# Paired steps on VectorE, streamed output weights and pooled weights transposed off TensorE in an attention + rational MLP kernel

## The chip, the cores and the metric

The kernel runs on one core of a Trainium2 chip. The metric is the device time of one execution in microseconds; the kernel before takes 930.41 us as the median of three runs (929.94 to 931.01). Engines are named as in the profile: PE is TensorE, PEld its weight loads, DVE is VectorE, ACT is ScalarE, POOL is GpSimd, SP is SyncE, which here only issues DMAs.

## The reference

Inputs are q, k, v of shape (8 batches, 8 heads, 576 tokens, 64), a 512x2048 matrix w_in, a 2048x512 matrix w_out and six coefficients. Everything is float32. Cut to what matters:

```python
# attention: a pooled part and a narrow local part, added
q_d, k_d, v_d = means of q, k, v over groups of 4 tokens          # 144 of 576
out_up    = repeat(softmax(q_d k_d^T / 8) v_d, 4)                 # back to 576
out_local = softmax(where(|i - j| < 4, q k^T / 8, -1e9)) v        # band of width 7
x = (out_up + out_local), heads side by side                      # 4608 x 512
# rational MLP
h = x @ w_in                                                      # 4608 x 2048
P = a0 + a1 h + a2 h^2 + a3 h^3
Q = 1 + |b0| |h| + |b1| h^2
out = (P / (Q + 1e-6)) @ w_out                                    # 4608 x 512
```

## The kernel before, in words

**The two products.** The 4608 tokens are cut into nine blocks of 512: blocks 0 to 7 hold the first 512 tokens of one batch each, block 8 the last 64 of all eight. A block has 16 steps; step n (0 to 143) computes h for 128 of the 2048 hidden columns. Float32 accuracy comes from splitting each operand into a high part that TensorE's one-pass float32 format holds and a low rest: three products (high x high, low x high, high x low) of four 128x512 matmuls, 12 per step (`h_part`, line L1389; in steps 0 to 15 it is four plain float32 matmuls instead, L1375). `middle(n)` turns the 128x512 h in PSUM into g and splits it: ScalarE reads h four times, VectorE runs seven operations of 512 columns (L1419 to L1437), ScalarE forms the reciprocal as exp(-ln Q) between them. `o_part(n, f)` multiplies g with 128 rows of w_out, again 12 matmuls (L1455), into four PSUM banks, one per 128 tokens, which gather all 16 steps of a block. `store` copies the four banks to SBUF, into the room of the block's high x (`xsf[blk.slot][0]`), and sends them out. So w_in and w_out stay in SBUF as high and low parts for the whole run, 16 tiles of 512 KB for each matrix.

**The attention** of batch b + 2 runs beside block b + 1. It goes by halves of a batch (`Half`: four heads as two pairs). Local scores of ten windows of 58 queries, a band mask, softmax; the local weights are transposed by VectorE (`flip`, L1129) from batch 2 on. VectorE's transpose works inside 32x32 blocks, so the blocks are brought to their partitions by four DMAs out to DRAM (`fd`, L1141) and one back (`ef`, L1146). Pooled scores use means of q and k (`pq`) that the DMA queues form: one load on SyncE (L524) and three that add on GpSimd's queue (L528); pooled values (`vpc`) come the same way. The pooled weights are transposed by TensorE, nine 112x112 transposes per half (`turn_pooled`, L1158) into PSUM, and ScalarE copies them out (L1170). `weight_both` (L754, L1209) multiplies all weights with v in one run of small matmuls, VectorE adds the two parts into x, and `split_x` makes its high and low part in four ScalarE and four VectorE operations per block.

**The order.** All work is handed to a list planner (`Plan`): each task has an engine, a cost, what it reads and writes, and a due time (`due_h(n)` for step n, with offsets such as `O_LAG`, `ENDS`, `SCORES_EARLY`). `Plan.run` gives each engine's free time to the open task with the earliest latest start, and the resulting order is written into the engines' queues; each queue keeps that order on the chip. `middle(n)` works in six tiles `mt` and four `gt`, two sets in turn:

```python
ta, tb, tq = (mt[2 * i + n % 2] for i in range(3))
gh, gl, u, log = rooms_g(n)
```

Of the kernel before, what the change touches and what calls it, by code (L numbers as in the profile page):

```python
# [2 lines left out]

# [25 lines left out]
QR = D + QC  # L29
BAND0 = 48  # L30
# [58 lines left out]
class Task:  # L89
    __slots__ = (  # L90
        "engine", "dur", "fn", "due", "preds", "succs", "late", "start", "end", "n", "lag", "uses", "load", "after",
        "loan", "step", "takes",
# [3 lines left out]
class Plan:  # L96
# [12 lines left out]
    def add(self, engine, dur, fn, reads=(), writes=(), due=None, lag=None, load=0.0, after=0.0):  # L109
# [4 lines left out]
        t.loan = next((w for w in writes if isinstance(w, Loan)), None) if engine == "PE" else None  # L114
        t.step = None
# [52 lines left out]
    def run(self):  # L168
        self.low, self.lent = 0, {}
        for t in reversed(self.tasks):  # L170
            late = 1e9 if t.due is None else t.due
            for s in t.succs:
                late = min(late, s.late - t.dur - self.gap(t, s))
            t.late = late
# [99 lines left out]
def attention_moe(  # L274
# [10 lines left out]
    band: bass.AP,  # L285
    out: bass.AP,
# [55 lines left out]
    mt = [put(f"m{i}", [P, DM], F32) for i in range(6)]  # L342
    gt = [put(f"g{i}", [P, DM], F32R) for i in range(4)]
    gb = [put(f"gb{i}", [P, DM], F32, g.at) for i, g in enumerate(gt)]
    ident = put("ident", [P, P], F32)
    identb = put("identb", [P, P], BF16)
    maskb = put("maskb", [P, 2, NW // 2 * D], BF16)
    maskd = put("maskd", [P, 2, NW // 2, QD], BF16)
# [9 lines left out]
    class Slot:  # L358


        def __init__(self, i, at=None):
# [8 lines left out]
            self.pq = one("pq", [P, 2, SD])  # L370
# [7 lines left out]
    class Pooled:  # L378


        def __init__(self, i, at=None):
            self.e = put(f"epc{i}", [P, NQ, NK, 2, D], F32, at)
            self.et = put(f"eptc{i}", [QR, NK * NQ, 2, QC], F32, self.e.at)
            keys = sorted(self.e.keys)
            self.rooms = [Room(None, keys[j::2]) for j in range(2)]

    pools = [Pooled(0)]
    slots = [Slot(i) for i in range(2)]
    vpc = put("vpc", [QR, 2, NK, D], F32)

# [17 lines left out]
    ]  # L408
    bounce = [[nc.dram_tensor(f"fd{i}_{j}", [4, QD, 4, NW // 2 * QD], F32, kind="Internal").ap() for j in range(2)] for i in range(2)]
# [44 lines left out]
    def weights(w, f, spot, due=None):  # L454
# [26 lines left out]
        if w or f >= NAT:  # L481
            parts(w, f)

# [10 lines left out]
    class Pair:  # L494
# [11 lines left out]
        def ep(self, i):  # L506
            return self.pool.e.ap[:, i, :, self.odd, :QC]

# [8 lines left out]
    def load_pooled(cs, values):  # L517

        b, q = cs[0].b, cs[0].i // 2
        loads = [(c.slot.pq, 0.5, [qkp[b, r, :, c.i] for r in range(POOL)]) for c in cs]  # L520
# [60 lines left out]
    def scores_pooled(cs, bk):  # L581
        def issue():
            for i in range(NQ):
                for n, c in enumerate(cs):
                    pq = flat(c.slot.pq.ap)
                    for j in range(2):
# [3 lines left out]
                            lhsT=pq[js, i * QC : i * QC + D],  # L590
                            rhs=pq[js, SD:],
# [3 lines left out]
        add("PE", 0.9 if cs[0].b == 0 else 1.15, issue, [c.slot.pq for c in cs], bk)  # L595
# [60 lines left out]
    def softmax_pooled(c, x, head=True):  # L656
# [17 lines left out]
        def exps():  # L674
            for i in range(NQ):
                nc.scalar.activation(  # L676
                    out=c.ep(i), in_=view[:, i, :].rearrange("p (n k) -> p n k", k=QC), func=AF.Exp,
# [151 lines left out]
    class Half:  # L829
# [22 lines left out]
        def scores(self, c, bk):  # L852
# [21 lines left out]
            add("PE", 0.95, issue, (c.slot.qk,), bk, due=self.due - SCORES_EARLY[c.odd] if c.b >= LATER else None)  # L874
# [22 lines left out]
        def scores_rest(self, bk):  # L897
# [21 lines left out]
            def pooled(i, j):  # L919
                js = slice(j * D, (j + 1) * D)  # L920
                for n, c in enumerate(self.cs):
                    pq = flat(c.slot.pq.ap)
                    nc.tensor.matmul(
                        bk[c.pos(j)].ap[n * D : (n + 1) * D, i * SD : (i + 1) * SD],
                        lhsT=pq[js, i * QC : i * QC + D],
                        rhs=pq[js, SD:],
# [3 lines left out]
            def issue():  # L930
# [17 lines left out]
                "PE", SREST, issue, (o.slot.qk, *(c.slot.pq for c in self.cs)), (*bk, bc),  # L948
                due=self.due - SCORES_EARLY[1]
# [78 lines left out]
        def pooled(self, bk):  # L1028
# [5 lines left out]
            if self.cs[0].b >= FLIP:  # L1034
# [3 lines left out]
                for c in self.cs:  # L1038
                    normalize(c, "pooled")
                return  # L1040
# [112 lines left out]

        def turn_pooled(self, bk):
# [27 lines left out]
        def weight_both(self, bk):  # L1182
# [15 lines left out]
            def issue():  # L1198
# [5 lines left out]
                for kc in range(NK):  # L1204
                    for h in range(2):
                        ks = slice(h * D, h * D + QC)
                        for n, c in enumerate(self.cs):
                            j = c.pos(h)
                            nc.tensor.matmul(  # L1209
                                bk[n].ap[j * D : (j + 1) * D, np_ : np_ + SD],  # L1210
                                lhsT=vpc.ap[ks, n, kc, :],
                                rhs=self.pool.et.ap[ks, kc * NQ : (kc + 1) * NQ, n, :],
# [7 lines left out]
            ready = [vpc, self.pool.et] + [c.slot.vw for c in self.cs] + [  # L1220
# [96 lines left out]
    def split_x(k, due=None):  # L1317
        blk = blocks[k]
        due = due or due_h(blk.first) - SPLIT_EARLY
        t = blk.t  # L1320
        for c in range(NCC):
            if blk.b is None:
                hi, lo = (tails(x, c) for x in blk.x)
                x = tails(xsf[blk.slot][1], c).ap
            else:
                hi, lo = (part(x, x.ap[:, c, :], 4 * c * t, 4 * t) for x in blk.x)
                x = xsf[blk.slot][1].ap[:, c, :]
            add("ACT", 0.11 + t / 1390, lambda hi=hi, x=x: nc.scalar.copy(out=hi.ap, in_=x), (lo,), (hi,), due=due)
            add(
                "DVE", 0.07 + t / 960,  # L1330
                lambda hi=hi, lo=lo, x=x: nc.vector.tensor_tensor(
                    out=lo.ap, in0=x, in1=hi.ap.bitcast(F32), op=ALU.subtract
                ),
                (lo, hi), (lo,), due=due,
            )
# [14 lines left out]
    def rooms_g(n):  # L1350
        k = n - blocks[-1].first
        k = k % 6 if k >= 0 else n % 2
# [52 lines left out]
    def middle(n):  # L1405

        ta, tb, tq = (mt[2 * i + n % 2] for i in range(3))
        gh, gl, u, log = rooms_g(n)
# [6 lines left out]
        read.append(act(0.66, gh, h, h.ap, AF.Identity, to=u, scale=a1, bias=a0))  # L1415
        v = nc.vector
        add(
            "DVE", 0.66,
            lambda: v.scalar_tensor_tensor(  # L1419
# [394 lines left out]
```

## Time and profile before

| what | value |
|---|---|
| runs, median (lowest to highest) | 930.41 us (929.94 to 931.01) |
| profiled execution, first to last instruction | 928.5 us |
| PE busy | 916.7 us (99%), 7129 matmul records |
| DVE busy | 859.7 us (93%) |
| ACT busy | 785.5 us (85%) |
| POOL busy | 117.7 us (13%) |
| DMA | 100.24 MB, mean 108 GB/s |
| granted TensorE clock | 1.00 |

The profiled execution's own time is its span; the page gives no time around it. Busy time is the union of an engine's instructions. The plain float32 matmuls of steps 0 to 15 have two records each. Small matmuls in different quarters of the array overlap, so their count says little; the time from one start to the next does.

### The profile page before, as it was taken

Reading aid. Unit: us, or ns where it says so; the run is one execution under the profiler, and the core shown is the slowest. Engines: PE = TensorE matmul, PEld = TensorE weight load, DVE = VectorE, ACT = ScalarE, POOL = GpSimd, SP = SyncE. Lnnn points to the kernel's source line nnn. Section 1 sums busy time; section 2 is a strip of 40 time slices with the busy share of each in tenths; the row PEclk is TensorE's granted clock in tenths of the full one; section 3 lists DMA queues with packets and bytes.
Section 4 is the critical chain, followed back from the end, with each engine's and each line's share of the span. In section 5 each row is a group of like instructions: output and inputs, shape, how many; then the busy total and the mean of one; then the engine's idle time right before and its main releaser. Section 6 shows DMA issues by size and latency. Waiting matters only on the chain.

```text
span 928.5 us, 19329 instructions
## 1 busy us (share of the span) xinstructions
PE 916.7 (99%) x7129; PEld 727.8 (78%) x7129; DVE 859.7 (93%) x1409; ACT 785.5 (85%) x1898; POOL 117.7 (13%) x140
## 2 busy tenths in 40 slices
PE   8999999999999999999999999999999999999998
PEld 6666667788888888788888888888888888888886
DVE  8899999999999998999999999999999989988994
ACT  5899997978897979888898979797989887678782
POOL 3122021202020202020112112021200000000000
PEclk9999999999999999999999999999999999999999
DMA  9987453636363634464455436463622110001001
GB/s 315 328 270 187 138 133 96 145 88 131 97 159 99 133 93 114 102 134 95 122 108 140 79 87 164 105 129 81 143 78 53 30 46 1 1 0 46 1 1 45
DMA packets 61853, 100.24 MB, mean 108 GB/s; under 512 B 8064, under 2 KB 41920, under 8 KB 61760
## 3 DMA queue, kind: packets, MB, share of 16 engines
q1 hardware_dynamic: 43888, 78.93, 26.6%
q0 software_dynamic: 17728, 19.96, 15.3%
q8 instruction: 56, 0.92, 0.4%
q14 instruction: 37, 0.30, 0.1%
q10 hardware_dynamic: 144, 0.13, 0.0%
HBM read 81.69 MB, written 17.30 MB: 107 GB/s over the span
## 4 chain that ended last, share of the span: by engine, by line
PE 75%; ACT 10%; DVE 10%; issue 3%; DMA 1%; SPq 0%; DVEq 0%; ACTq 0%
PE psum L1455 34%; PE psum L1389 33%; ACT m L1403 3%; ACT gb L1403 1%; PE psum L754 1%; ACT el L648 1%; DVE g L1428 1%; DVE m L1431 1%; ACT epc L676 1%; DVE m L1436 1%; DVE m L1419 1%; PE psum L1158 1%; PE psum L1209 1%; PE psum L1375 1%; PE psum L911 1%
## 5 line engine op out<-in xcount | busy, mean ns | idle before, releaser
L1455 PE MATMUL psum<-wh,g 128*128 128x512 f32 x1072 | 367.3, 403 | 2.7 <-DVE g L1428 1.4
L1389 PE MATMUL psum<-xs,wh 128*128 128x512 f32 x1024 | 256.9, 391 | 0.2 <-DVE xf L804 0.2
L1403 ACT ACTIVATE m<-psum,cf 128x512 f32<-128x512 f32 x288 | 217.4, 760 | 44.8 <-PE psum L1389 37.3
L1455 PEld LDWEIGHTS psum<-wh,g 128*128 128x128 f32 x1072 | 200.0, 188 | 54.8 <-issue 5.7
L1389 PEld LDWEIGHTS psum<-xs,wh 128*128 128x128 f32 x1024 | 191.0, 188 | 40.9 <-DVE xf L804 0.7
L1455 PE MATMUL psum<-wl,g 128*128 128x512 f32 x536 | 209.3, 390 | 0.0
L1389 PE MATMUL psum<-xs,wl 128*128 128x512 f32 x512 | 137.1, 390 | 0.0
L1403 ACT ACTIVATE gb<-psum,cf 128x512 f32<-128x512 f32 x134 | 109.7, 819 | 16.4 <-PE psum L1455 15.5
L1403 ACT ACTIVATE gb<-m,cf 128x512 f32<-128x512 f32 x134 | 101.7, 759 | 21.1 <-DVE m L1419 16.3
L1455 PEld LDWEIGHTS psum<-wl,g 128*128 128x128 f32 x536 | 100.7, 188 | 22.1 <-issue 2.3
L1428 DVE TENSOR_TENSOR g<-m,m 128x512 fp32r<-128x512 f32 x134 | 92.3, 689 | 23.4 <-ACT m L1403 17.3
L1389 PEld LDWEIGHTS psum<-xs,wl 128*128 128x128 f32 x512 | 96.0, 188 | 20.0
L1419 DVE SCALAR_TENSOR_TENSOR m<-m,cf,m 128x512 f32<-128x512 f32 x144 | 107.3, 745 | 2.4 <-ACT m L1403 2.1
L528 POOL DMA_DIRECT2D pq<-in_qkp_dram x84 | 75.9, 958 | 218.4 <-DMA pq<-in_qkp_dram 178.2
L1403 ACT ACTIVATE m<-gb 128x512 f32<-128x512 f32 x134 | 89.1, 665 | 14.7 <-DVE m L1424 12.5
L1436 DVE TENSOR_TENSOR m<-m,m 128x512 f32<-128x512 f32 x144 | 98.9, 687 | 2.4
L1424 DVE TENSOR_TENSOR m<-m,m 128x512 f32<-128x512 f32 x144 | 98.1, 681 | 0.1
L1425 DVE TENSOR_TENSOR m<-m,gb 128x512 f32<-128x512 f32 x134 | 91.9, 686 | 4.2
L1437 DVE TENSOR_TENSOR g<-m,m 128x512 fp32r<-128x512 f32 x134 | 91.6, 684 | 3.0
L1431 DVE SCALAR_TENSOR_TENSOR m<-m,g 128x512 f32<-128x512 f32 x134 | 91.8, 685 | 2.0
L1403 ACT ACTIVATE m<-psum 128x512 f32<-128x512 f32 x144 | 89.6, 622 | 0.0
L528 POOL DMA_DIRECT2D vpc<-in_vp_dram x42 | 35.2, 837 | 360.6 <-DMA vpc<-in_vp_dram 218.9
(120 smaller groups left out, 1056.2 us busy)
## 6 DMA issues: line engine op xcount, KB each, us to landing
qk<-in_qk_dram SPq DMA_DIRECT2D x32, 590.0 KB, 4.3
pq<-in_qkp_dram POOLq DMA_DIRECT2D x84, 144.0 KB, 4.0
vw<-in_vw_dram SPq DMA_DIRECT2D x32, 320.0 KB, 4.1
out_dram<-xf SPq DMA_DIRECT2D x35, 256.0 KB, 3.3
fd<-fx SPq DMA_DIRECT2D x96, 80.0 KB, 2.2
ef<-fd SPq DMA_DIRECT2D x24, 320.0 KB, 3.0
vpc<-in_vp_dram POOLq DMA_DIRECT2D x42, 168.0 KB, 3.5
sx<-in_w_in_dram SPq DMA_DIRECT2D x5, 1024.0 KB, 11.1
```

Source lines behind the costliest of these rows:

```text
L528: lambda d=dst, x=x: nc.gpsimd.dma_start(out=d.ap, in_=x, accum_op=ALU.add),
L648: nc.scalar.activation(out=dst, in_=src, func=AF.Exp, bias=nm[:, 5 * j + k : 5 * j + k + 1], scale=scale, accum_out=sm[:, n : n + 1],)
L1389: nc.tensor.matmul(ph.ap[:, f * t : (f + 1) * t], lhsT=(high, low)[j][0][fc].ap[:, c, :], rhs=blk.x[i].ap[:, c, :] if blk.b is not None el ...
L1403: return add("ACT", cost, lambda: nc.scalar.activation(out=to, in_=in_, func=func, **kw), (room_in, cf, *more), (out_,))
L1419: lambda: v.scalar_tensor_tensor(out=tb.ap, in0=tq.ap, scalar=b1, in1=tb.ap, op0=ALU.mult, op1=ALU.add),
L1424: add("DVE", 0.61, lambda: v.tensor_tensor(out=ta.ap, in0=ta.ap, in1=tq.ap, op=ALU.mult), (ta, tq), (ta,))
L1425: add("DVE", 0.61, lambda: v.tensor_tensor(out=ta.ap, in0=ta.ap, in1=u, op=ALU.add), (ta, gh), (ta,))
L1428: add("DVE", 0.61, lambda: v.tensor_tensor(out=gh.ap, in0=ta.ap, in1=tq.ap, op=ALU.mult), (ta, tq), (gh,))
L1431: lambda: v.scalar_tensor_tensor(out=tb.ap, in0=tb.ap, scalar=CONE, in1=gh.ap.bitcast(F32), op0=ALU.add, op1=ALU.mult),
L1436: add("DVE", 0.61, lambda: v.tensor_tensor(out=tb.ap, in0=ta.ap, in1=tb.ap, op=ALU.subtract), (ta, tb), (tb,))
L1437: add("DVE", 0.61, lambda: v.tensor_tensor(out=gl.ap, in0=tb.ap, in1=tq.ap, op=ALU.mult), (tb, tq), (gl,))
L1455: nc.tensor.matmul(ob[sub].ap, lhsT=g[i].ap[:, f0 : f0 + P], rhs=flat((high, low)[j][1][fc].ap), start=(fc == 0 and m == 0), stop=(fc == N ...
```

## The change

- **Two steps per VectorE operation.** In steps 14 to 127 `middle` writes ScalarE's four reads into halves of 1024-wide tiles, and the odd step of a pair runs the seven VectorE operations, the logarithm and the exponential once for both (`rational(..., 2)`). There are two sets of wide tiles in turn. Steps 0 to 13 and block 8 stay single.
- **Streamed w_out.** Pairs of 128-row chunks are a unit. Units 0 and 1 stay resident (`KEPT = 2`). The six others are copied to DRAM once (`keep_out`, SyncE), and from block 1 on each is fetched again for each block by two 512 KB DMAs on GpSimd's queue (`fetch_out`) into one of two rooms in turn (units 6 and 7). The rooms of units 2 to 5 become the second set of wide tiles, second g tiles, a tile for u, and the output staging.
- **Own rooms for output staging** (`leave`), outside the x buffers.
- **Pooled weights transposed by VectorE** for batches 3 to 7 (`PFLIP = 3`): one 128x1152 transpose in place per half, four DMAs out to DRAM and one back (`flip_pooled`); `turn_pooled` is left out there. For these batches the host lays pooled q, k and v out in two blocks of 24 of 32 columns (`qkb`, `vp`), with 56 rows per matmul instead of 48.
- `split_x` works in two pieces per block instead of four. `Plan.run` now repeats its planning 400 times on the host with random changes of priority and keeps the order whose last TensorE task ends first. Dues and offsets are changed.

```diff
+    def unit(k, fc):
+        i = fc // 2
+        if k and i >= KEPT:
+            i = NFC // 2 - 2 + (k * (NFC // 2 - KEPT) + i - KEPT + UNIT0) % 2
+        return i
+    def keep_out(i):
+        for j, x in enumerate((high2[1][i], low2[1][i])):
+            add("SP", 1.7, lambda d=scratch[i][j], x=x: nc.sync.dma_start(out=d, in_=x.ap.bitcast(F32)), (x,), (held((i, j)),), due=KEEPDUE)
+    def fetch_out(k, i, due):
+        n = unit(k, 2 * i)
+        for j, x in enumerate((high2[1][n], low2[1][n])):
+            add(
+                "POOL", 1.0, lambda d=scratch[i][j], x=x: nc.gpsimd.dma_start(out=x.ap.bitcast(F32), in_=d),
+                (held((i, j)),), (x,), due=due, lag=4.0, load=1.7,
+            )
...
                 for c in self.cs:
                     normalize(c, "pooled")
+                if self.cs[0].b >= PFLIP:
+                    self.flip_pooled()
                 return
...
+        def flip_pooled(self):
+            pool, q = self.pool, self.cs[0].i // 2
+            e = pool.eb.ap.rearrange("p h b i k c -> p (h b) (i k c)")
+            flat_e = pool.eb.ap.rearrange("p h b i k c -> p (h b i k c)")
+            add("DVE", 1.4, lambda: nc.vector.transpose(out=flat_e, in_=flat_e), (*pool.rooms, pool.e), (*pool.rooms, pool.e))
+            d = bouncep[q]
+            def leave():
+                for a in range(4):
+                    rows = slice(a * QD, (a + 1) * QD)
+                    nc.sync.dma_start(out=d[:, :, a].rearrange("m k n -> k m n"), in_=e[rows])
+            def back():
+                nc.sync.dma_start(out=pool.eb.ap.rearrange("p n b i k c -> p (n b i k c)"), in_=d.rearrange("m k a n -> (m k) (a n)"))
+            there = Room(None, [("D", "p", q)])
+            add("SP", FLIPSP, leave, (*pool.rooms, pool.e), (there,), lag=FLIPLAG[2])
+            add("SP", 1.2, back, (there,), (*pool.rooms, pool.e), lag=FLIPLAG[3])
...
             if b >= FLIP:
-                half_.turn_pooled(bk)
+                if b < PFLIP:
+                    half_.turn_pooled(bk)
...
     def middle(n):
-        ta, tb, tq = (mt[2 * i + n % 2] for i in range(3))
-        gh, gl, u, log = rooms_g(n)
+        pair = PAIRS[0] <= n < PAIRS[1]
+        odd = n // 2 % 2 if pair else 0
+        ta, tb, tq = (mt[odd][2 * i + n % 2] for i in range(3))
+        gh, gl, u, log = rooms_g(n) if not pair else (us[n % 2], None, us[n % 2].ap, None)
...
+        if not pair:
+            rational(ta, tb, tq, gh, gl, gh, u, log, 1)
+        elif n % 2:
+            rational(*wide[odd], *gt2[2 * odd : 2 * odd + 2], line, flat(line.ap), flat(logs[odd].ap), 2)
...
+        if k and fc % 2 == 0 and fc // 2 >= KEPT and subs[0] == 0:
+            fetch_out(k, fc // 2, due - FETCH)
...
-                        rhs=flat((high, low)[j][1][fc].ap),
+                        rhs=weight_out(k, fc, j).ap,
...
+            room = leave[sub]
+            osb = room.ap
...
+PAIRS = (14, 128)
+KEPT = 2
+KEEPDUE = 307.365
+FETCH = -15.499
-O_LAG = 2.09
+O_LAG = 4.049
-H_STEP = 6.1
+H_STEP = 5.979
-ENDS = (7.3, 45.2)
+ENDS = (11.53, 52.06)
+PFLIP = 3
```

## Rows read from the trace of the kernel before

**Rows 1.** The page: span, and busy time of each engine.

```profile
span 928.5 us, 19329 instructions
PE 916.7 (99%) x7129; PEld 727.8 (78%) x7129; DVE 859.7 (93%) x1409; ACT 785.5 (85%) x1898; POOL 117.7 (13%) x140
```

**Rows 2.** Windows: length, busy (xcount) of PE, PEld, DVE, ACT, POOL, clock, DMA, GB/s.

```profile
146.00:172.00 26.00, 24.64 (x207) 19.49 (x196) 25.83 (x42) 22.19 (x69) 0.82 (x1) 1.00 0.40 116
172.00:738.00 566.00, 565.65 (x4694) 463.99 (x4693) 535.58 (x904) 496.18 (x1296) 85.42 (x99) 1.00 0.47 108
```

**Rows 3.** The chain that ended last, in time: start, duration, what.

```profile
305.28 2.72 PE psum L1389 x12
308.00 2.72 PE psum L1455 x12
...
404.93 2.72 PE psum L1389 x12
```

**Rows 4.** Line L1158: duration ns min/median/max, first and last start.

```profile
L1158 PE MATMUL psum<-ident,epc x108: 257/259/260, 181.0 to 730.4; 112*112 112x112 f32 x108
```

**Rows 5.** Timeline of PE, first half: start, duration, what.

```profile
523.04 0.39 PE L1455 MATMUL psum<-wh,g 128*128 128x512 f32 x1
...
525.77 0.93 PE L1158 MATMUL psum<-ident,epc 112*112 112x112 f32 x8
...
532.28 0.81 PE L869 MATMUL psum<-qk 64*64 64x64 f32 x40
533.02 2.12 PE L1389 MATMUL psum<-xs,wh 128*128 128x512 f32 x8
...
535.97 0.93 PE L754 MATMUL psum<-ef,vw 64*64 64x64 f32 x48
```

**Rows 6.** Timeline of PE, second half.

```profile
577.96 0.39 PE L1455 MATMUL psum<-wh,g 128*128 128x512 f32 x1
...
586.52 0.81 PE L869 MATMUL psum<-qk 64*64 64x64 f32 x40
```

**Rows 7.** Groups by line: count, busy us, mean ns, idle before.

```profile
L1424 DVE TENSOR_TENSOR m<-m,m 128x512 f32<-128x512 f32 x144 | 98.1, 681 | 0.1
...
L1129 DVE STREAM_TRANSPOSE fx<-eq 128x640 f32<-128x640 f32 x24 | 20.1, 837 | 0.4 <-DMA out_dram<-xf 0.4
...
L489 DVE TENSOR_TENSOR wl<-wb,wh 128x1024 fp32r<-128x1024 f32 x16 | 19.4, 1213 | 0.6 <-ACT wh L487 0.6
```

**Rows 8.** Issues of the outgoing detour DMAs: duration ns min/median/max.

```profile
L1141 SPq DMA_DIRECT2D fd<-fx x96: 302/444/1673, 167.6 to 722.0; - x96
```

**Rows 9.** DMA issues: count, KB each, median us to landing.

```profile
qk<-in_qk_dram SPq DMA_DIRECT2D x32, 590.0 KB, 4.3
...
fd<-fx SPq DMA_DIRECT2D x96, 80.0 KB, 2.2
ef<-fd SPq DMA_DIRECT2D x24, 320.0 KB, 3.0
...
sl<-in_w_out_dram SPq DMA_DIRECT2D x3, 1024.0 KB, 15.7
```

**Rows 10.** The chain in time, where VectorE is on it.

```profile
147.81 1.13 DVE wl L489
148.94 0.60 DVE m L1431
```

**Rows 11.** Timeline of PE at its longest wait after 146 us.

```profile
165.94 1.07 PE L1389 MATMUL psum<-xs,wl 128*128 128x512 f32 x4
168.38 0.50 PE L1455 MATMUL psum<-wh,g 128*128 128x512 f32 x1 [1.36 <-DVE g L1428]
```

**Rows 12.** GpSimd: all vpc issues (ns min/median/max), and two on its timeline.

```profile
L528 POOL DMA_DIRECT2D vpc<-in_vp_dram x42: 817/819/1197, 46.7 to 702.7; - x42
501.04 0.82 POOL L528 DMA_DIRECT2D vpc<-in_vp_dram  x1 [3.22 <-DMA vpc<-in_vp_dram]
504.87 0.82 POOL L528 DMA_DIRECT2D vpc<-in_vp_dram  x1 [3.02 <-DMA vpc<-in_vp_dram]
```

More of the change, by code (lines that the diff above doesn't have):

```diff
@@ L168, in run, with again, push, once @@
     def run(self):
+        kept = [(t, dict(t.preds), list(t.succs), t.lag) for t in self.tasks]
+        def again():
+            for t, preds, succs, lag in kept:
+                t.preds, t.succs, t.lag, t.start = dict(preds), list(succs), lag, None
+            return self.once()
+        dice = random.Random(SEED)
+        best, bias = None, [0.0] * len(kept)
+        for n in range(PASSES):
+            for t, x in zip(self.tasks, bias):
+                t.bias = x
+            if n:
+                self.push(dice)
+            tried = [t.bias for t in self.tasks]
+            again()
+            cost = max(t.end for t in self.tasks if t.engine == "PE")
+            if best is None or cost <= best:
+                best, bias = cost, tried
+        for t, x in zip(self.tasks, bias):
+            t.bias = x
+        return again()
+    def push(self, dice):
+        line = {}
+        for t in sorted(self.tasks, key=lambda t: t.start):
+            line.setdefault(t.engine, []).append(t)
+        before = {y: x for ts in line.values() for x, y in zip(ts, ts[1:])}
+        gaps = [y for x, y in zip(line["PE"], line["PE"][1:]) if y.start - x.end > 0.1 and y.start > PUSHED]
+        if not gaps:
+            return
+        for t in dice.sample(gaps, min(len(gaps), dice.choice((1, 2, 4)))):
+            step = dice.choice((1.0, 3.0, 8.0))
+            for _ in range(dice.choice((2, 5, 10))):
+                at = max(t.preds, key=lambda p: p.end + self.gap(p, t), default=None)
+                if at is None or at.engine == "PE" and t.engine != "PE":
+                    break
+                t = at
+                t.bias -= step
+                ahead_ = before.get(t)
+                ready = max((p.end + self.gap(p, t) for p in t.preds), default=0.0)
+                if ahead_ is not None and t.start > ready + 0.05 and dice.random() < 0.5:
+                    ahead_.bias += step
+    def once(self):
         self.low, self.lent = 0, {}
@@ L387, in attention_moe @@
     pools = [Pooled(0)]
-    slots = [Slot(i) for i in range(2)]
-    vpc = put("vpc", [QR, 2, NK, D], F32)
+    assert maskd.at - ident.at >= 8 * (NQ * D + SD)
+    slots = [Slot(i, None, (pq0, None)[i]) for i in range(2)]
+    vpc = put("vpc", [VR, 2, NK, D], F32)
     half = NFC // 2
@@ L482, in weights @@
             parts(w, f)
+        if w and f // 2 >= KEPT:
+            keep_out(f // 2)
     def parts(w, f, due=None):
@@ L1319, in split_x, with some @@
         due = due or due_h(blk.first) - SPLIT_EARLY
[L1320 to L1328, printed above, removed]
-            add(
-                "DVE", 0.07 + t / 960,
-                lambda hi=hi, lo=lo, x=x: nc.vector.tensor_tensor(
-                    out=lo.ap, in0=x, in1=hi.ap.bitcast(F32), op=ALU.subtract
+        n = blk.t if blk.b is not None else B * REST
+        hi, lo = blk.x
+        x = xsf[blk.slot][1]
+        def some(r, k):
+            return part(r, flat(r.ap)[:, 2 * k * n : 2 * (k + 1) * n], 8 * k * n, 8 * n)
+        for k in range(NCC // 2):
+            add(
+                "ACT", 0.11 + 2 * n / 1390, lambda k=k: nc.scalar.copy(out=some(hi, k).ap, in_=some(x, k).ap),
+                (some(lo, k),), (some(hi, k), hi), due=due,
+            )
+        for k in range(NCC // 2):
+            add(
+                "DVE", 0.07 + 2 * n / 960,
+                lambda k=k: nc.vector.tensor_tensor(
+                    out=some(lo, k).ap, in0=some(x, k).ap, in1=some(hi, k).ap.bitcast(F32), op=ALU.subtract
                 ),
-                (lo, hi), (lo,), due=due,
+                (lo, some(hi, k)), (some(lo, k), lo), due=due,
             )
@@ L1575, in attend @@
     def attend(b):
+        if b == PFLIP:
+            own = pools[0]
+            pads = own.eb.ap.rearrange("p h b i k c -> p (h b i k) c")[:, :, QB:]
+            add("POOL", 0.5, lambda: nc.gpsimd.memset(pads, 0.0), (), (own.e, *own.rooms))
         early, gap = (SPLIT_EARLY, QUAD_GAP) if b < LATER else ENDS
```

185 lines of the change are left out of this document (135 added, 50 removed).

## The prediction

> **What bounds the kernel now.** I read the busy table first [rows 1]: TensorE is busy 916.7 of 928.5 us, so at most 11.8 us is waiting. Busy time of pipelined matmuls can hide slack, so I went to the windows by stage [rows 2]: TensorE idles 1.36 us between 146 and 172 us and 0.35 us in the 566 us from 172 to 738. The granted clock is 1.00 (2.4 GHz) in both, so the clock has nothing to give back. VectorE is busy 535.6 of the same 566 us, ScalarE 496.2, the DMA engines 0.47 of the time. The chain of waits shows the pattern there [rows 3]: twelve matmuls of the first product (L1389), then twelve of the second (L1455), each group 2.72 us, no gap; the same place comes back one batch (16 steps) later, after 404.93 - 305.28 = 99.65 us. So from 172 us on the kernel is one full queue on TensorE: a step costs 5.44 us, and the attention put between costs its own time plus the switches. An edit pays there only if it takes work off TensorE; it harms if it starves it.
>
> **Part 1, pooled weights transposed by VectorE.** For batches 3 to 7 (ten halves of four heads) the nine matmul transposes (L1158) per half go. The kernel has 108 of them [rows 4], nine in each of 12 halves; the 18 of batch 2 stay. I price a half by TensorE's starts. In the first half shown, 9.24 us pass from 523.04 to 532.28 [rows 5]; they hold 36 large matmuls, 3 x 2.72 = 8.16 us undisturbed [rows 3], so 1.08 us is left for transposes and switches. A little of that stays, because the score matmuls at 532.28 still end the run: an interruption costs 535.97 - 533.02 - 2.72 = 0.23 us in both its switches [rows 5], and about 0.1 of it is the entry that remains. The saving is 1.0 us. In the second half 8.56 us pass from 577.96 to 586.52 [rows 6], with 32 large matmuls, 32 x 2.72/12 = 7.25 us; 1.31 less 0.1 is 1.2 us. Per batch 2.2, for five batches **11.0 us** on the path that sets the end.
>
> In its place VectorE gets ten transposes of 128x1152. The trace has 128x640 at 837 ns [rows 7]; bounds are that and twice that, I take 837 x 1152/640 = 1.5 us, 3.0 per batch. SyncE gets four DMAs out and one back per half, like the existing detour of the local weights: 0.44 us an issue [rows 8], 2.2 us to land, then 3.0 us back [rows 9]. The chain is 1.5 + 4 x 0.44 + 2.2 + 0.4 + 3.0 = 8.9 us; before, 535.97 - 525.77 = 10.2 us lay between the first transposes and the run that uses them [rows 5]. It fits with 1.3 us to spare, so I charge nothing. The DMA back waits at the head of SyncE's queue for the landing, 2.2 us; behind it stand loads of later halves and output stores, which nothing on TensorE waits for within such a time. ScalarE loses the copies out of PSUM, off the path. The pooled operands get longer columns (56 deep instead of 48) but no more of them: nothing.
>
> **Part 2, two steps per VectorE operation** (steps 14 to 127, 57 pairs). Seven operations of 512 columns, twice, become seven of 1024. By mean durations two of 0.681 become one of 1.213 us [rows 7], saving 0.15. But neighbours overlap: in the chain one of 512 holds the engine 0.60 us and one of 1024 1.13 [rows 10], saving 0.07. So a pair frees 0.5 to 1.0 us of VectorE, a batch (8 pairs) 4 to 8, of which the new transposes take 3.0 back. VectorE now idles 566.0 - 535.6 = 30.4 us in 5.7 batches, 5.3 each; the batch gets 2.2 us shorter, so 4 to 8 us per batch stay idle: it is not the bound after either, and as TensorE waited 0.35 us there, this part gains nothing after 172 us. If that cover were gone, each further us of VectorE would be a us of the end. The price of pairing is latency: the second product waits for two steps and runs about four behind the first instead of two. A pair needs two VectorE and two ScalarE operations before its first matmul and three more before its last, 5 to 8 us at 1.13 each, against 6 x 2.72 = 16 us of other groups in that lag: hidden.
>
> Before 172 us pairing can gain. TensorE stood 1.36 us before 168.38 for VectorE's L1428 [rows 11]; start to start it lost 168.38 - 165.94 - 4 x 0.227 = **1.5 us**. With four steps of lag that wait goes, and no longer wait stands beside it in this stage's window, so I count it as gained.
>
> **Part 3, streamed w_out.** From batch 1 on, 6 units of two 512 KB tiles come per block through GpSimd's queue: 6.3 MB per block, 50 MB in eight. At 97 us a block that is 65 GB/s beside the window's 108; share 0.47 x 173/108 = 0.75, so the engines can carry it [rows 2]. Two rooms alternate: a room is free from the last matmul of its unit until its turn two units later, three groups of L1389 and two of L1455, 5 x 2.72 = 13.6 us [rows 3]. The fetch needs two issues of 0.82 us [rows 12] and a landing. No row shows 512 KB on this queue; the nearest is 590 KB on SyncE's at 4.3 us, the far end 1024 KB at 15.7 in the crowded start [rows 9]. I take 4.3: 5.9 us, hidden with 7.7 to spare; at the far end (2 x 1.20 + 15.7 = 18.1) a unit would be 4.5 us late. A fetch that waits for its room stands at the head of GpSimd's queue; behind it stand the pooled additions, whose last on vpc is issued at 504.87 [rows 12] for a use at 536: with 27 us to spare, a few reach nobody. The twelve copies out are SyncE issues, in front of loads for batch 2.
>
> The Trainium skill, page "SBUF — State Buffer" (section "SBUF: two separate sides"), speaks against this part: a DMA issued from GpSimd can't write its descriptors while VectorE runs an operation in a mode that takes both ports, and the page reports about 3.1 us where 0.62 is normal. The trace does not bear so large a factor out for this mix of operations: 42 issues took 817 ns at least, 819 in the median and 1197 at most, with VectorE 95% busy [rows 2, 12]. Estimated with the page's factor of five, two issues would take 8 us and the fetch 12.5, inside 13.6 by 1 us; by that rule the late fetch below would deserve a chance of 0.25, at the same time.
>
> **Part 4, own rooms for output staging, wider splits, new priorities.** Staging frees VectorE's transposes from outgoing stores; TensorE's idle time after 172 us shows no such wait: nothing. The splits of x in two instead of four operations save VectorE 0.3 us per block: hidden. New dues and the search over orders add no instruction. A better order can gain 0.35 us after 172 us; a worse one can lose, and the nearest row is the stall of 1.5. I take 0, ends -0.35 and +4 (some three such stalls).
>
> **Sum.** The profiled execution spans 928.5 us and the trace shows no time around it; the median of the runs, 930.4, is 1.9 above. 928.5 - 11.0 - 1.5 = 916.0 us of span, 917.9 us as a run.
>
> **Rivals.** *The transition stalls.* The second set of rooms for pairs lies in w_out units 2 to 5, which must first be copied out (eight of twelve tiles, 4.2 MB) and used. At 116 GB/s for a share of 0.40 [rows 2] the engines have 174 to spare, so 24 us; TensorE has about five groups, 13.6 us, to fill it. Price once 10 us: 928. For it: VectorE is 99% busy there; against: a tile can leave as soon as it is split. *The pooled chain is late.* Its margin is 1.3 us, and each wait on SyncE adds to it. If a half loses 1.2 us the gain is gone: 930. Against: the plan can put the run that uses it later. *The fetch is late (the slower case).* GpSimd's queue keeps order; a fetch placed behind a chain of three additions waits for three landings, 3.22 + 0.82 us each [rows 12], 12.1 us, plus its own 5.9: 18.0 against 13.6, TensorE stands 4.4 us. In every second of 12 halves that is 26 us: 944; it decides from 1.05 us per half on, where the 12.5 us are eaten. For it: the queue idles on just such waits; against: 7.7 us of margin where no chain is ahead. *More is gained*: VectorE, freed earlier, also removes waits before 146 us, 911 to 914.
>
> **How the numbers follow.** Forecast 0.58 (914 to 922), more gained 0.04, transition 0.13 (925 to 928), pooled chain 0.09 (929 to 932), late fetch 0.16 (above 932). Faster by over 0.2% (1.9 us, about what a measurement of this kernel can tell from no change): 0.58 + 0.04 + 0.13 = 0.75; within it 0.09; slower 0.16. The range 912 to 932 leaves out the late fetch and part of the larger gain.
>
> **What would show it.** Right: 18 transposes left on TensorE; groups still at 2.72 us and a batch of 97.4 us; TensorE idle below 1 us after 172; fetches landed within 8 us of their issue; VectorE's share below 0.946. Wrong: TensorE waiting for a DMA into w_out or for the pooled DMA, a stall of several us between 126 and 200 us, or a batch that stays at 99.65.

## The result, and the profile after

The changed kernel takes 918.94 us (median of 4 runs, 918.72 to 919.54) against 930.37 us (929.94 to 931.01): a ratio of 0.9878, 95% interval 0.9864 to 0.9892, or 11.4 us less. The forecast was 917.9. Below, the page of the changed kernel (it answers [rows 1]), then its windows (columns as in [rows 2]): the start of block 0's work, the transition, and the long stretch.

```profile
span 917.2 us, 18534 instructions
PE 905.3 (99%) x7039; PEld 718.6 (78%) x7039; DVE 836.4 (91%) x1004; ACT 749.0 (82%) x1738; POOL 171.9 (19%) x237
```

```profile
60.00:105.00 45.00, 42.79 (x326) 26.08 (x324) 44.06 (x70) 44.97 (x113) 8.28 (x9) 1.00 0.89 262
...
146.00:172.00 26.00, 26.00 (x179) 20.81 (x178) 25.28 (x30) 25.26 (x68) 7.74 (x11) 1.00 0.79 194
...
172.00:738.00 566.00, 566.00 (x4609) 464.89 (x4608) 530.87 (x587) 469.62 (x1150) 120.16 (x164) 1.00 0.72 198
```

TensorE idles 0.00 us from 146 to 738 us (1.36 + 0.35 before), VectorE's share from 172 to 738 us is 530.87 / 566 = 0.938 (0.946 before), and the DMA share there rose from 0.47 to 0.72. A busy TensorE says little, so I count what it got done: the same window for the large matmuls alone, first the second product, then the first one, after and then before (columns: length, PE busy (xcount), PEld busy (xcount), clock, DMA share, GB/s).

```profile
172.00:738.00 566.00, 286.49 (x1128) 209.43 (x1128) 1.00 0.72 198
...
172.00:738.00 566.00, 280.61 (x1116) 208.17 (x1115) 1.00 0.72 198
```

```profile
172.00:738.00 566.00, 270.99 (x1094) 201.56 (x1093) 1.00 0.47 108
...
172.00:738.00 566.00, 265.85 (x1092) 203.84 (x1092) 1.00 0.47 108
```

That is 1128 + 1116 = 2244 large matmuls; the kernel before shows 1094 + 1092 = 2186 in the same 566 us. The 58 more are worth 58 x 2.72 / 12 = **13.1 us**. From the starts of all matmuls between 172 and 740 us: the small ones and the transposes took 59.7 us before and 49.5 after (-10.2), and what the large ones took beyond 2.72/12 us each, mostly at switches, fell from 11.7 to 8.4 (-3.3), with 72 switches between large and small instead of 118. Of the 10.2 us some 1.6 only moved ahead of 172 us: nine transposes of batch 2, 40 local score matmuls and four mask matmuls. The transition gave 1.3 more; block 0 gave back 3.1 (below). Together -11.7, for 11.3 us of span.

Two places after: the transposes left on TensorE (answers [rows 4]), the local score matmuls (L1041) from one batch to the next, in two windows; each row has count, duration in ns as minimum/median/maximum, first and last start.

```profile
L1314 PE MATMUL psum<-ident,epc x18: 257/259/260, 162.7 to 211.7; 112*112 112x112 f32 x18
...
L1041 PE MATMUL psum<-qk x84: 216/218/268, 484.8 to 582.0; 64*64 64x64 f32 x84
...
L1041 PE MATMUL psum<-qk x40: 216/218/267, 581.9 to 583.2; 64*64 64x64 f32 x40
```

A batch takes 581.9 - 484.8 = 97.1 us, where 99.65 stood [rows 3].

### The profile page after: what moved, and what is told of

Same layout as the page of the kernel before. It is cut to its first block, busy times and chain, and to the rows that moved or that the text cites. A ratio compares the mean times of both kernels' runs of the same rounds, so it can differ in the third digit from the quotient of the medians.

```text
span 917.2 us, 18534 instructions
## 1 busy us (share of the span) xinstructions
PE 905.3 (99%) x7039; PEld 718.6 (78%) x7039; DVE 836.4 (91%) x1004; ACT 749.0 (82%) x1738; POOL 171.9 (19%) x237
## 4 chain that ended last, share of the span: by engine, by line
PE 90%; ACT 7%; DVE 2%; issue 1%; DMA 1%; SPq 0%; DVEq 0%
PE psum L1639 41%; PE psum L1560 38%; PE psum L1546 3%; ACT m L1574 2%; PE psum L884 2%; ACT gb L1574 1%; PE psum L1372 1%; ACT el L775 1%; PE psum L1041 1%; PE psum L999 1%; PE psum L1052 1%; DMA qk<-in_qk_dram 1%; ACT wh L596 1%; ACT epc L806 1%; ACT sl L573 0%
## 5 line engine op out<-in xcount | busy, mean ns | idle before, releaser
L1639 PE MATMUL psum<-wh,gg 128*128 128x512 f32 x912 | 297.4, 393 | 0.0
L1639 PEld LDWEIGHTS psum<-wh,gg 128*128 128x128 f32 x912 | 169.3, 188 | 36.2 <-DVE gg L1619 0.2
L1639 PE MATMUL psum<-wl,gg 128*128 128x512 f32 x456 | 177.6, 389 | 0.0
L1574 ACT ACTIVATE m<-psum,cf 128x512 f32<-128x512 f32 x172 | 128.4, 755 | 40.8 <-PE psum L1560 35.0
L1574 ACT ACTIVATE n<-psum,cf 128x512 f32<-128x512 f32 x116 | 86.3, 752 | 53.6 <-PE psum L1560 48.9
L1639 PEld LDWEIGHTS psum<-wl,gg 128*128 128x128 f32 x456 | 85.6, 188 | 17.8
L1574 ACT ACTIVATE line<-psum,cf 128x512 f32<-128x512 f32 x114 | 91.1, 800 | 0.4 <-DVE m L1607 0.4
L656 POOL DMA_DIRECT2D vpc<-in_vp_dram x42 | 36.6, 872 | 242.8 <-DMA vpc<-in_vp_dram 231.6
L1603 DVE SCALAR_TENSOR_TENSOR m<-m,cf,m 128x512 f32<-128x512 f32 (+1 forms) x58 | 58.1, 1002 | 18.2 <-ACT m L1574 18.0
L1122 ACT ACTIVATE eq<-eq,nmb 128x64 f32<-128x64 f32 x200 | 66.8, 343 | 2.4 <-DVE nmb L1116 2.4
L1639 PE MATMUL psum<-wh,g 128*128 128x512 f32 x160 | 56.8, 420 | 0.6 <-DVE g L1619 0.6
L1618 DVE TENSOR_TENSOR m<-m,m 128x512 f32<-128x512 f32 (+1 forms) x58 | 54.8, 945 | 1.0
L1606 DVE TENSOR_TENSOR m<-m,m 128x512 f32<-128x512 f32 (+1 forms) x58 | 54.5, 940 | 0.1
L1574 ACT ACTIVATE m<-psum 128x512 f32<-128x512 f32 x86 | 53.5, 623 | 0.5 <-PE psum L1560 0.5
```

Of the source, the lines that this page charges most:

```text
L656: lambda d=dst, x=x: nc.gpsimd.dma_start(out=d.ap, in_=x, accum_op=ALU.add),
L1122: nc.scalar.activation(out=e[:, n], in_=e[:, n], func=AF.Exp, bias=nm[:, n : n + 1], scale=scale, accum_out=sm[:, n : n + 1],)
L1574: return add("ACT", cost, lambda: nc.scalar.activation(out=to, in_=in_, func=func, **kw), (room_in, cf, *more), (out_,))
L1603: lambda: v.scalar_tensor_tensor(out=tb_, in0=tq_, scalar=b1, in1=tb_, op0=ALU.mult, op1=ALU.add),
L1606: dve(0.61, lambda: v.tensor_tensor(out=ta_, in0=ta_, in1=tq_, op=ALU.mult), (ta, tq), (ta,))
L1618: dve(0.61, lambda: v.tensor_tensor(out=tb_, in0=ta_, in1=tb_, op=ALU.subtract), (ta, tb), (tb,))
```

## The experiments

The theory first: the gain is the transposes that left TensorE; pairs and streaming are hidden. Its rival: the pairs pay, through VectorE. Both fell in part, so the reasons were formed anew after the first four runs. "After" is 918.9 us, "before" 930.0 beside these runs. TensorE's idle and the large matmuls done are those of 172 to 738 us (large matmuls: 2186 before, 2244 after). Idle is what the overlapping ends of the matmuls leave of a stall, so the count of large matmuls says more: in run 5, 33 fewer of them are 7.5 us beside 3.4 us of idle.

| version | us | ratio to before (95%) | idle | large done |
|---|---|---|---|---|
| 1 transposes back | 928.6 | 0.9987 (0.9978-0.9995) | 0.1 | 2201 |
| 2 no pairs | 930.2 | 1.0006 (0.9992-1.0020) | 5.7 | 2197 |
| 3 transposes alone | 957.2 | 1.0289 (1.0275-1.0303) | 18.3 | 2121 |
| 4 block 0's old lag | 921.9 | 0.9907 (0.9893-0.9922) | 0.0 | 2243 |
| 5 VectorE loaded | 926.9 | 0.9965 (0.9953-0.9977) | 3.4 | 2211 |
| 6 fetch twice | 1057.8 | 1.1364 (1.1332-1.1397) | 86.1 | 1809 |
| 7 as 3, old dues | 932.9 | 1.0031 (1.0020-1.0042) | 7.8 | 2184 |
| 8 all, old dues | 934.7 | 1.0046 (1.0034-1.0058) | 9.1 | 2185 |
| 9 as 7, VectorE spared | 929.5 | 0.9995 (0.9987-1.0004) | 5.9 | 2197 |
| 10 first order | 922.0 | 0.9913 (0.9900-0.9926) | 0.0 | 2242 |
| 11 longer search | 919.1 | 0.9895 (0.9876-0.9914) | 0.0 | 2243 |
| 12 operations split | 920.1 | 0.9893 (0.9877-0.9910) | 0.4 | 2238 |

**1. Transposes back on TensorE in four of five batches.**

```diff
-PFLIP = 3
+PFLIP = 7
```

> The changed kernel with one number moved (PFLIP 3 to 7), so that four of the five changed batches (8 of 10 half pairs) have their pooled weights transposed on TensorE again; pairs, streaming and rooms stay. Theory (the gain is the transposes, with what each of their switches costs TensorE): 8/10 of 11.0 us comes back, 918.9 + 8.8 = 927.7 us (926 to 929), and the 18 transposes of the trace become 90. Rival (the gain is VectorE's relief by pairs): VectorE keeps its pairs and even loses its square transposes, so 917 to 920.5 us.

Measured: 928.6, so 9.7 us came back, as the theory said. The 18 transposes became these:

```profile
L1314 PE MATMUL psum<-ident,epc x90: 257/259/260, 167.6 to 607.9; 112*112 112x112 f32 x90
```

TensorE stays full (idle 0.1 us) and gets 43 fewer large matmuls done, 43 x 2.72 / 12 = 9.7 us. Read the other way, it tells more: pairs, streaming, rooms, new due times and one batch's transposes together gain 1.3 us (with due times made for the whole).

**2. No pairs; 3. the transposes alone.** Both make every step a VectorE operation of its own; version 3 also keeps as much of w_out as the kernel before (KEPT) and has the old staging rooms.

```diff
-PAIRS = (14, 128)
+PAIRS = (14, 14)
-O_LAG = 4.049
+O_LAG = 2.09
...
-KEPT = 2
+KEPT = 8
```

> The changed kernel with every step its own VectorE operation again (PAIRS 14 to 14, and the lag of the second product back to its old value), while VectorE still makes the pooled transposes and 12 of 16 chunks of w_out still come through GpSimd's queue. Theory (pairs are hidden under TensorE from 172 us on): 917 to 921 us, the higher end if the stall at 166 to 168 us of the kernel before returns; VectorE's share in 172 to 738 us rises above 0.95 and TensorE's idle stays under 1.5 us there. Rival (VectorE, then over 0.96 of that stretch, becomes the bound without pairs): 924 us or more, with waits of TensorE on VectorE's rational function from 172 us on.

> Part 1 alone: the pooled weights transposed by VectorE, but no pairs, no streaming of w_out (all that the kernel before kept stays kept) and the old staging rooms. Theory: 930.4 - 11.0 = 919.4 us (918 to 922), so that at least 8.5 of the 11.4 us gained come from this part. Rival (the parts need each other: VectorE has no room for the square transposes without pairs): 924 to 931 us, with VectorE as what TensorE waits for between 172 and 738 us.

Measured: 930.2 and 957.2. The theory missed both: run 2 falls to its rival, and run 3 is slower than either range. The saving is there (start to start, what is left of the transposes takes 0.7 and 1.5 us from 172 to 740 us, 10.0 before), but stalls eat it. The long stretch of version 2, then TensorE's longest waits in version 3 (columns: total us, times, longest):

```profile
172.00:738.00 566.00, 560.29 (x4528) 457.26 (x4531) 540.02 (x898) 480.05 (x1235) 119.36 (x162) 0.99 0.73 196
```

```profile
PE psum L1625 <- DVE g L1596: 8.8, 6, 3.5
PE psum L1625 <- ACT xf L1669: 5.4, 3, 2.2
PE psum L1625 <- DVE g L1605: 3.5, 4, 1.4
PE psum L1546 <- ACT m L1560: 3.4, 3, 2.4
```

L1625 is the second product there, which waits for VectorE's g and for ScalarE's staging copies (xf). So either VectorE lacked time, or the order didn't fit. Versions 5, 7, 8, 9 and 12 are to tell these apart.

**4. Block 0 in its old lag.**

```diff
-        due = due_h(n) + O_LAG * H_STEP + 0.25 * f
+        due = due_h(n) + (O_LAG if n >= PAIRS[0] else 2.09) * H_STEP + 0.25 * f
```

> The changed kernel with the lag of the second product in block 0 alone set back to its old value (2.09 steps of the first product in place of 4.05), the rest as changed. Theory (the three stalls of TensorE at 65.9, 75.5 and 100.6 us, 0.98 + 1.70 + 0.71 us less what a matmul takes, come from the larger lag, which leaves TensorE with nothing but first products that wait for ScalarE): they go, 916 to 917.5 us. Rival (ScalarE is the bound of 60 to 105 us in whatever order): they stay or move to 105 to 146 us, 918.5 to 920.5 us.

The stalls meant are these of the changed kernel (timeline of TensorE: start, duration, what [idle before]):

```profile
66.86 0.47 PE L1639 MATMUL psum<-wh,g 128*128 128x512 f32 x1 [0.59 <-DVE g L1619]
...
77.19 0.70 PE L1546 MATMUL psum<-xf,wb 128*128 128x512 f32 x1 [1.30 <-ACT gb L1574]
...
101.34 0.70 PE L1546 MATMUL psum<-xf,wb 128*128 128x512 f32 x1 [0.32 <-ACT gb L1574]
```

Measured: 921.9, worse than both expectations. The three stalls go (60 to 146 us: busy 85.96 of 86.00, 83.78 after), and block 0 gets its work done: from 45 to 146 us 112 records of the float32 first product (0.43 us each) and 156 other large matmuls (0.227), 83.4 us in all, against 80.3 after (106 and 154) and 83.3 before (106 and 167). But two other stalls come: one at 39 us, before any second product has started (TensorE's wait, then the window around it, columns as in [rows 2]), and one at the transition:

```profile
PE psum L1546 <- DVE xf L912: 2.0, 1, 2.0
...
30.00:45.00 15.00, 13.01 (x251) 8.26 (x251) 10.64 (x18) 10.50 (x19) 3.60 (x5) 0.89 0.91 300
...
146.18 0.46 PE L715 MATMUL psum<-pq 64*64 64x144 f32 x2 [0.22 <-ACT eq L775]
148.33 1.16 PE L715 MATMUL psum<-pq 64*64 64x144 f32 x22 [1.69 <-ACT eq L775]
149.42 3.60 PE L1560 MATMUL psum<-xs,wh 128*128 128x512 f32 x8
```

Eight large matmuls that take 1.98 us elsewhere in the trace took 3.60, at a mean granted clock of 0.69 from 150 to 155 us, after 1.9 us of standing: the wait cost its own length and 1.6 us of clock. The wait at 39 us is 0.9 us in the changed kernel, and the clock around it 1.00. Counted in the same way, run 4 loses 2.6 us up to 45 us and 4.3 at the transition and gains 3.0 between: 3.9 us, as its span does (921.1 for 917.2). The profiled execution is the slowest of four; the one at a mean clock of 1.00 took 920.1. So the lag does cost block 0 some 3 us, but its old value, with the other due times as changed, loses more elsewhere.

**5. VectorE loaded, in the same order.** One operation of every third pair is done twice.

```diff
+        rep = 1 + (w == 2 and next(heavy) % 3 == 0)
         dve(
-            0.61, lambda: v.tensor_tensor(out=gl_, in0=tb_, in1=tq_, op=ALU.mult),
+            0.61, lambda: [v.tensor_tensor(out=gl_, in0=tb_, in1=tq_, op=ALU.mult) for _ in range(rep)],
```

> The changed kernel in the same order, pairs kept, but in every third pair VectorE does its last operation (1024 columns, some 1.2 us) twice: 19 more operations, 23 us of VectorE in all, about 16 of them in 172 to 738 us, which takes its share there from 0.938 to about 0.966, as high as without pairs. Theory, new since pairs turned out to be needed (what pairs pay is VectorE's time: at such a share its lateness reaches TensorE): 925 to 932 us, with TensorE waiting for g several times after 172 us. Rival (what pairs pay is their second set of rooms and the lag of four steps, VectorE's time has slack): 918.5 to 921 us and TensorE idle under 1 us in 172 to 738.

Measured: 926.9, 8.0 us for 858.0 - 836.4 = 21.6 us of VectorE. It looks like the theory, but five waits for the pairs' g (gg) hold 2.2 us in all:

```profile
PE psum L1645 <- DVE gg L1623: 1.2, 3, 0.6
PE psum L1645 <- DVE gg L1612: 1.0, 2, 0.8
```

The added operation sits at the end of a chain, so this run doesn't part time from lateness; run 12 does, for about half of what pairs save.

**6. Each fetch of a w_out tile issued twice.** The second waits for the first, as both write the same room.

```diff
-                "POOL", 1.0, lambda d=scratch[i][j], x=x: nc.gpsimd.dma_start(out=x.ap.bitcast(F32), in_=d),
+                "POOL", 1.0, lambda d=scratch[i][j], x=x: [nc.gpsimd.dma_start(out=x.ap.bitcast(F32), in_=d) for _ in range(2)],
```

> The changed kernel in the same order, with each fetch of a w_out tile issued twice (same data, same room), so a unit takes four issues of about 0.65 us and 2 MB in place of two and 1 MB, and 50 MB more are moved in all. Theory (the fetch has about 7 us of margin): about 1.3 us of issues and 4 to 5 us of transfer more, still inside 13.6 us: 918.5 to 922 us. Rival (the fetch is near its limit, or the DMA engines are: their share goes from 0.74 to about 0.95): 930 us or more, with TensorE waiting for w_out tiles after 172 us.

Measured: 1057.8, far beyond the rival. The expectation had left out that a wait holds GpSimd's queue. Its timeline there, and what TensorE then waits for:

```profile
260.91 0.89 POOL L443 DMA_DIRECT2D wl<-ws  x1
267.47 0.55 POOL L443 DMA_DIRECT2D wl<-ws  x1 [5.67 <-DMA wl<-ws]
268.00 0.54 POOL L443 DMA_DIRECT2D wh<-ws  x1
272.97 0.53 POOL L443 DMA_DIRECT2D wh<-ws  x1 [4.43 <-DMA wh<-ws]
```

```profile
PE psum L1639 <- DMA wh<-ws: 101.0, 16, 15.2
```

One unit holds the queue from 260.91 to 273.5 us, 12.6 us, with the next fetch and the pooled loads behind it. The DMA engines are not the limit (their share is 0.73 to 0.77 from 172 to 738 us). This is the late fetch of the prediction's rivals, made to happen by another cause: a wait at the head of one queue, and 101 us of TensorE's waiting in 16 places.

**7. The transposes alone, with the old due times; 8. all parts, with the old due times.**

```diff
-DUES = (-5.76, -9.77, ...)
+DUES = (0.0,) * 12
-LEADS = (0.17, 10.7, ...)
+LEADS = (0.0,) * 12
-H_FIRST = 5.91
+H_FIRST = 6.27
-H_STEP = 5.979
+H_STEP = 6.1
...
```

SPLIT_EARLY, ENDS, SCORES_EARLY, LATE, AHEAD and ROOM go back in the same way.

> The transposes alone again (no pairs, no streaming, old staging rooms), this time with every due time set back to what the kernel before had, so that the order is not one made for pairs. Theory (VectorE needs the pairs to have room for the transposes): slower than the changed kernel still, 926 to 940 us, with waits on VectorE's g after 172 us. Rival (the 957 us of the first try came from due times made for another kernel): 918 to 922 us, the 11.0 us of my sum.

> The changed kernel, all its parts kept (pairs with their lag, streaming, transposes, the search), with the other due times and the offsets per half set back to the values of before. Theory (dues add nothing, the parts pay): 917 to 922 us. Rival (the tuned offsets carry a good part of the gain, and a bad order loses what the transposes save): 925 to 935 us, with stalls of TensorE spread over the batches.

Measured: 932.9 and 934.7. In run 7 the transposes, priced at 11.0 us, gain nothing without pairs: the time is in the theory's range, though not for its reason, as run 9 shows. Run 8 falls to its rival: with nearly the same instructions as after, and VectorE less busy (514.4 of 566 us), the due times alone cost 15.7 us. Where it goes, in run 7 and then in run 8:

```profile
567.83 0.85 DVE L1246 STREAM_TRANSPOSE fx<-eq 128x640 f32<-128x640 f32 x1 [1.73 <-DMA out_dram<-xf]
...
569.68 0.68 DVE L1596 TENSOR_TENSOR g<-m,m 128x512 fp32r<-128x512 f32 x1
...
570.42 0.49 PE L1625 MATMUL psum<-wh,g 128*128 128x512 f32 x1 [0.81 <-DVE g L1596]
```

```profile
561.15 1.38 DVE L1291 STREAM_TRANSPOSE epb<-epb 128x1152 f32<-128x1152 f32 x1 [0.33 <-ACT epb L848]
...
562.16 2.03 ACT L1685 COPY lv<-psum 128x512 f32<-128x512 f32 x4
...
569.03 0.80 ACT L1574 ACTIVATE line<-psum,cf 128x512 f32<-128x512 f32 x1
...
569.88 1.65 PE L1560 MATMUL psum<-xs,wh 128*128 128x512 f32 x3 [3.10 <-ACT line L1574]
```

In run 7 VectorE stands 1.73 us for an outgoing store that still reads the staging room, and the g behind it comes 0.81 us late. In run 8 a half's transposes, its softmax and the block's four output copies fall together, and ScalarE empties a PSUM bank 3.10 us late; of the 9.1 us that TensorE idles in this stretch of run 8, 7.8 end with such a read by ScalarE (L1574). Neither is a lack of VectorE's time over the stretch: work bunched in front of a step's chain made it late.

**9. As 7, with VectorE spared.**

```diff
-        dve(0.61, lambda: v.tensor_tensor(out=ta_, in0=ta_, in1=u, op=ALU.add), (ta, ru), (ta,))
+        cut = slice(0, 320 if w == 1 else 1024)
+        dve(0.61, lambda: v.tensor_tensor(out=ta_[:, cut], in0=ta_[:, cut], in1=u[:, cut], op=ALU.add), (ta, ru), (ta,))
```

> The transposes alone with the old due times (932.9 us) once more, in the same order, but VectorE spared: one of its seven operations per step, the addition in the rational function, works on 320 of 512 columns, and the sum of the other 192 is left out. That takes some 0.2 us x 144 = 29 us off VectorE, what the pairs save in the changed kernel (865.7 - 836.4 us of busy time). Theory (without pairs VectorE's time is what eats the transposes' gain): the stalls on VectorE go and 9 to 11 us come free: 920 to 924 us. Rival (the order and the single set of rooms cause the stalls, whatever VectorE's load): 930 to 933 us.

Measured: 929.5. VectorE is 864.6 - 838.5 = 26 us less busy, and the end comes 3.4 us earlier. That is below the rival's range by half a microsecond and far from the theory's. Of the nine places from 172 to 738 us at which TensorE loses over half a microsecond from one large matmul's start to the next (325.8 to 733.4 us in run 7), seven stay, at 324.4 to 713.8 us, and VectorE's wait for outgoing stores stays (3.8 us, 3.0 in run 7).

**10. The first order; 11. a longer search.**

```diff
-PASSES = 400
+PASSES = 1
```

(1500 in run 11.)

> The changed kernel with the first order that its priorities give, without the search over 400 pushed orders; due times as changed. Theory (the due times carry the order, the search trims gaps): 919 to 922 us. Rival (the search is what fits the new mix of work together, as the old due times, which cost 15 us even with the search, suggest): 925 us or more, with stalls spread over the batches.

> The changed kernel with 1500 pushed orders tried in place of 400, from the same seed. Theory (TensorE idles 0 us from 146 to 738 us, so what an order can still give are the three stalls before 105 us, which the search does not touch, and a few switches): 917.5 to 919.5 us, no difference to tell. Rival (the order still holds switches and stalls that matter): 915 to 917.5 us.

Measured: 922.0, at the edge of the theory's range, and 919.1, the theory. The search is worth 3.1 us, and more of it nothing that can be told. TensorE's idle from 172 to 738 us is 0.00 in both. What the search found lies mostly ahead of that: run 10 idles 1.17 us from 146 to 172 us, and has done 244 large matmuls by then where the changed kernel has done 254 (2.3 us).

**12. The pairs' operations split, all else kept.** Each VectorE operation on 1024 columns is issued as two on 512.

```diff
+        class Halves:
+            def __getattr__(self, name):
+                def run(**kw):
+                    for j in range(w):
+                        cut = slice(j * DM, (j + 1) * DM)
+                        getattr(nc.vector, name)(**{
+                            k: x[:, cut] if w == 2 and k in ("out", "in0", "in1") else x for k, x in kw.items()
+                        })
+                return run
-        v = nc.vector
+        v = Halves()
```

> The changed kernel in the same order, with the rooms, the lag and the paired ScalarE operations of the pairs, but each of VectorE's seven operations on 1024 columns issued as two on 512: what a pair saves VectorE is given back (57 x 7 operations, by the earlier profiles 865.7 - 836.4 = 29 us in all, about 0.5 us per pair), and nothing else. Theory (what Part 2 pays is VectorE's time in an order that has little room for it, as 23 us of added work cost 8.0 us): 926 to 930 us. Rival (what it pays is the second set of rooms and the lag; the added work hurt because it stood at the end of single chains): 919 to 921.5 us, with TensorE's idle under 1 us in 172 to 738 us.

Measured: 920.1, the rival. The long stretch:

```profile
172.00:738.00 566.00, 565.64 (x4603) 463.66 (x4602) 543.64 (x916) 470.41 (x1154) 119.42 (x163) 1.00 0.71 198
```

VectorE is busy 543.64 / 566 = 0.960 of it, more than without pairs (540.0), and TensorE idles 0.4 us instead of 5.7. What was given back is 852.4 - 836.4 = 16 us and not 29, since the two halves of an operation don't depend on each other and overlap (the second starts 0.60 us after the first, which takes 0.68); it cost 1.1 us. So what pairs pay is for the most part not VectorE's bulk time: about half of it given back costs 1.1 us (run 12), and 26 us spared without pairs bring 3.4 (run 9). The other half was not given back in any run.

## Why the prediction was right, and where it was not

**Part 1, 11.0 us.** Right in kind and, if anything, a little small: run 1 gives back 9.7 us for eight halves, 1.2 each where the sum has 1.1. But the term was written as if it stood alone, and it doesn't: runs 2, 3 and 7 have the transposes off TensorE as well (0.7 to 1.5 us left of 10.0) and no gain in time.

**Part 1's detour** was the step that failed worst. I charged nothing because a chain of 8.9 us fitted a gap of 10.2. The chain takes 11.0 to 18.2 us (start of VectorE's transpose to landing of the DMA back, ten halves, median 14.3):

```profile
L1291 DVE STREAM_TRANSPOSE epb<-epb x10: 1335/1375/1379, 257.4 to 703.3; 128x1152 f32<-128x1152 f32 x10
L1299 SPq DMA_DIRECT2D fp<-epb x40: 303/460/1289, 258.9 to 706.0; - x40
DMA to landing us min/median/max: 2.1/4.6/8.4
L1302 SPq DMA_DIRECT2D epb<-fp x10: 326/337/426, 265.3 to 710.6; - x10
DMA to landing us min/median/max: 3.7/5.3/8.6
```

The transpose is as priced (1.38 us for 1.5); the landings are 4.6 and 5.3 us where I took 2.2 and 3.0 from [rows 9]. There are two reasons. Those rows move 80 and 320 KB, the new DMAs 144 and 576. And run 7 has the same detour without the streaming:

```profile
fp<-epb SPq DMA_DIRECT2D x40, 144.0 KB, 2.5
epb<-fp SPq DMA_DIRECT2D x10, 576.0 KB, 4.8
```

So the way back was mis-sized by its length (4.8 us without streaming), and the way out grew beside the streaming (2.5 to 4.6); even without it the chain takes 8.9 to 11.7 us, median 10.7, more than the gap in seven of ten halves. With the gap as it was, this would have been the rival "the pooled chain is late". It did no harm, because the matmuls that use the result now come 19 to 24 us after the transpose and have 2.2 to 11.8 us in hand. I had taken a gap of the old order as fixed.

**Part 2** as a matter of VectorE's time: right as far as it was tested, a cover that isn't used up (run 12). "If that cover were gone, each further us of VectorE would be a us of the end" was not: 16 us cost 1.1, 26 us spared gave 3.4, and 21.6 us at the end of chains cost 8.0. The 1.5 us at the transition came (146 to 172 us has no idle), but "no longer wait stands beside it" overlooked block 0, whose second product is also held four steps: its three stalls and slower first products lost 3.1 us, and the old lag gives 3.0 of work back there (run 4). I had put the lag down to steps 14 on only.

**Part 3** was right. Fetches land 3.3 to 10.0 us after issue, so "within 8 us" was missed by the slowest:

```profile
L443 POOL DMA_DIRECT2D wh<-ws x48: 530/546/1240, 156.8 to 899.3; - x48
L443 POOL DMA_DIRECT2D wl<-ws x48: 530/551/1262, 157.4 to 898.4; - x48
...
DMA to landing us min/median/max: 3.3/5.0/10.0
```

From a unit's first issue to its last landing 5.4 to 14.4 us pass (median 8.0, 5.9 forecast), and the first matmul that uses it comes 0.9 to 36.6 us later (48 units, median 7.9). Two units of 48 had no more than 1.0 us. The rival was nearer than its 0.16 suggests: run 6 shows what lies behind that edge. The Trainium skill, page "SBUF — State Buffer" (section "SBUF: two separate sides"), has GpSimd kept from writing descriptors while VectorE runs an operation in a mode that takes both ports; the prediction's estimate of 12.5 us put the page's factor of five on every issue. With VectorE 94% busy, 96 issues took 0.55 us in the median and 1.26 at most, so no issue here was slowed so far; which operations would run in such a mode, no run shows.

**Part 4** was mis-sized. "I take 0, ends -0.35 and +4": measured on the full change, old due times cost 15.7 us and the order's search is worth 3.1. The value 0 held because the order in the change fits it; the bound of +4 for one that doesn't was four times too small, and 934.7 lies outside the range given. The staging rooms, priced at nothing, end a wait that shows only where the rest is tight: VectorE stands 3.0 us in 172 to 738 us for outgoing stores in run 7 and 7.1 in run 3, 0.4 before, and none after.

**What stays open.** The parts don't add: the transposes alone gain nothing (run 7), the rest with one batch of them 1.3 us (run 1), all together 11.4. Runs 2, 7 and 8 each take away something that the order needs, and 9 and 12 speak against VectorE's bulk time as the main reason, 12 with about half of it. Which of the rest it is, the second set of rooms, the lag of four steps or due times made for them, is not shown: no run has an order tuned for transposes without pairs, nor single operations in the pairs' rooms with their own chains, nor the new search on the kernel before. The sum came out within 1.0 us partly by luck: the long stretch gained 13.1 us where the sum had 11.0, and block 0 lost 3.1 that it did not have.

## What to carry to other kernels

Work taken off the engine that binds is a saving only as far as the order lets the others deliver in time. Price it with the gap that the new order will have, and re-time the whole before judging one part alone. When a relief of an engine is to explain a gain, give the time back in the same order: here 16 us cost 1.1. On a queue that keeps its order, look at how long one wait holds it, not at bytes.

## What the runs showed that was not expected

Two VectorE operations on 512 columns that don't depend on each other cost less than their durations: 57 x 7 splits added 16 us of busy time, 0.04 us each, where 2 x 0.685 - 1.22 = 0.15 was the difference of the means.

A wait can cost more than itself through the clock: in run 4, 1.9 us of standing was followed by eight matmuls in 3.60 us instead of 1.98. Its 1.99 us of standing at 39 us was followed by eight float32 records in 5.40 us; in run 3, 2.00 us at the same place was followed by eight in 3.70. In run 6 the clock was 0.50 (1.2 GHz) from 276 to 282 us, where TensorE had stood 10.49 us. In the changed kernel 1.30 us of standing at 77 us left it at 1.00.
